# Three steps regrouped ahead of the score writes, and unused products on TensorE in the opening of a talking-heads attention and expert-layer kernel

## The chip, the cores and the metric

One core of one Trainium2 chip runs the whole program. The metric is the device time of one execution in microseconds (us). Five engines work side by side, each through its own list of instructions in order: TensorE (PE; its weight loads are shown apart as PEld), VectorE (DVE), ScalarE (ACT), GpSimd (POOL, here only an issuer of DMAs) and SyncE (SP, an issuer of DMAs). Sixteen DMA engines move the data.

## The reference

Inputs are q, k and v of shape (4, 12, 448, 64), two 12x12 head mixers, and the weights of two layers. In short:

```
scores = q @ k^T / 8                       # per batch and head, 448 x 448
scores = einsum("bhij,hg->bgij", scores, w_pre)
attn   = softmax over j of scores
attn   = einsum("bhij,hg->bgij", attn, w_post)
x      = (attn @ v) as 1792 rows x 768
x      = ((x @ w1) * (x @ w2)) @ w3 @ w_out
out    = max(x @ m1, x @ m2, x @ m3) @ m_out
```

The result is float32. The dense products are made from operands cut into a high and a low part (`hi`, `lo`), three products for each.

## The kernel before, in words

**Scores.** `unit(b, r, u)` (L331) multiplies 128 query rows (block r) of one pair of heads u with the keys `kall` into a PSUM room ("m", "p" or "s"), and ACT or DVE copies it out with the scale. For batch 0, block 0 the copies go to one wide row tile, `at` (called `a` in the trace, its six parts `("arow", u)`), all others to one of two tiles `st` (called `s`), and from both a DMA on SP writes them to `sdram`. The write of `at` leaves out the first FIRST rows (L365).

**Regrouping.** The head mixers need rows ordered by (query, head). `regroup(b, p)` (L373) builds the tile `x` of step p, 20 queries of 12 heads. It reads `sdram` with two DMAs, except for steps below FIRST of batch 0, which it copies out of `at` directly with four DMAs of 5 queries x 12 heads, 60 rows of 1792 bytes each (L384). There are three `x` tiles (AHEAD + 1).

**Steps.** `softmax` (L396) mixes heads on PE (`m<-x,kp`, L407), takes the negated maximum on DVE (`nmax`, L411) and the exponential on ACT (L414). `post` (L430) mixes again (L445) and copies the result into `at` over the rows; so this copy is planned after all readers of the rows. `attend` (L467) multiplies with v.

**Fusion and dense layers.** `fuse_parts` (L564) multiplies w3 with w_out (L605), in groups of 24 products (four pieces of six) that end in one of two PSUM banks `pw`; the first group uses `pw[0]`, the second `pw[1]`. Its operands arrive as 64-bit floats by DMAs of POOL and are made into float32 pairs by ACT and DVE (`convert`, L503, then L570/L571 for w_out and L535/L537 for w3). Six w_out buffers (`early`) and three w3 buffers (`wraw`) go round, so a load waits for a conversion. Dense layers for batches 0 and 1 follow between the attention steps (L685), and the last two batches come at the end (L221).

**The order.** Every piece is given to a planner (`Plan`, L67) with an engine, a cost, a key and what it reads and writes. `order` (L89) simulates the engines: each takes its ready piece with the lowest key; a load is started when the simulated pipe is less than BACK = 2.5 us behind, at RATE = 0.29 MB per us and LAND = 2.0 us to land; at most 8 loads of an engine are in flight. The instructions are emitted in that order, so each engine's list is fixed in advance, and a piece that is late on the chip holds what stands behind it on its engine. The pieces of the opening come from `attention_parts` (L1045): keys and queries, six units of block 0, then the regroups of the first two steps (L1063), then the second block of queries (L1065), then the loop over steps.

Of the kernel before, what the change touches and what calls it, by code (L numbers as in the profile page):

```python
# [18 lines left out]
P = 128  # L19
GI = 10  # L20
# [10 lines left out]
AHEAD = 2  # L31
# [3 lines left out]
HP = H // 2  # L35
# [22 lines left out]
SWITCH = 0.21  # L58
LAND = 2.0
RATE = 0.29  # L60
FIRST = 2 * 2 * GI
BACK = 2.5
STAY = 0.5
QUEUED = 8
# [2 lines left out]
class Plan:  # L67

    def __init__(self):
        self.ops, self.wrote, self.read = [], {}, {}  # L70

    def __call__(self, eng, took, key, do, reads=(), writes=(), bytes=0, mode=None):
        deps = set()
# [15 lines left out]
    def order(self):  # L89

        n = len(self.ops)
        after, left = [[] for _ in range(n)], [0] * n
        for x, op in enumerate(self.ops):
            left[x] = len(op[3])
            for d in op[3]:
                after[d].append(x)
        ready = {e: [] for e in ENGINES}
        loads = []
        busy = {e: False for e in ENGINES}
        taken, out, events = [False] * n, [], []  # L100
        mode, pipe = None, 0.0
        flying = {e: 0 for e in ENGINES}

        def offer(x):
            if self.ops[x][4]:
                heapq.heappush(loads, (self.ops[x][1], x))
                return
            for e in self.ops[x][0]:
                heapq.heappush(ready[e], (self.ops[x][1], x))

        for x in range(n):
            if not left[x]:
                offer(x)
        now, wake = 0.0, -1.0
        while True:
            later = []
            while loads and pipe - now < BACK:
                key, x = heapq.heappop(loads)
                (e, took), = self.ops[x][0].items()
                if busy[e] or flying[e] == QUEUED:  # L120
                    later.append((key, x))
                    continue
                busy[e] = True
                flying[e] += 1
                out.append((x, e, now))
                pipe = max(pipe, now + took) + self.ops[x][4] / RATE / 1e6
                heapq.heappush(events, (now + took, 0, x, e))
                heapq.heappush(events, (pipe + LAND, 1, x, None))
            for y in later:
                heapq.heappush(loads, y)  # L130
            if loads and pipe - now >= BACK and wake <= now:
                wake = pipe - BACK + 0.01
                heapq.heappush(events, (wake, 2, -1, None))
            for e in ENGINES:
                while not busy[e] and ready[e]:
                    if e == "PE":
                        best = min(ready[e], key=lambda r: (r[0] + STAY * (self.ops[r[1]][5] != mode), r[1]))
                        ready[e].remove(best)
                        heapq.heapify(ready[e])
                        x = best[1]  # L140
                    else:
                        _, x = heapq.heappop(ready[e])
                    if taken[x]:
                        continue
                    taken[x] = True
                    took, m = self.ops[x][0][e], self.ops[x][5]
                    if e == "PE" and m != mode:
                        took, mode = took + SWITCH, m
                    busy[e] = True
                    out.append((x, e, now))  # L150
                    heapq.heappush(events, (now + took, 0, x, e))
                    heapq.heappush(events, (now + took, 3, x, e))
                    heapq.heappush(events, (now + took + HOP, 1, x, e))
            if not events:
                break
            now, kind, x, e = heapq.heappop(events)
            if kind == 1 and self.ops[x][4]:
                flying[next(iter(self.ops[x][0]))] -= 1
            if kind == 0:
                busy[e] = False  # L160
            elif kind != 2:
                for y in after[x]:
                    same = e is not None and not self.ops[y][4] and list(self.ops[y][0]) == [e]
                    if same == (kind == 3):
                        left[y] -= 1
                        if not left[y]:
                            offer(y)
        assert len(out) == n, (len(out), n)
        self.end = now
        return out  # L170

# [6 lines left out]
def attention_talking_heads_moe_kernel(  # L178
# [16 lines left out]
    nc = tc.nc  # L195
# [128 lines left out]
    def load_q(b, r, key, eng="SP", after=()):  # L324
# [3 lines left out]
            3072 * w, list(after), [("q", slot)])  # L328
        return slot

    def unit(b, r, u, slot, key, room="s"):  # L331

        whole = P * (r + 1) <= S
        parts = [(u, 0), (u, HB)] if whole else [(2 * u, 0), (2 * u + 1, 0)]
        pt = {"m": pm, "p": pp, "s": pz}[room]

        w = min(P, S - P * r)
        q = qs[slot].rearrange("p x j -> p (x j)")[:, :HP * w].rearrange("p (x j) -> p x j", x=HP)

        def multiply(_):  # L340
            for c, (pr, i) in enumerate(parts):
                for o in range(2):
                    sl = slice(o * D, (o + 1) * D)
                    nc.tensor.matmul(  # L344
                        pt[HB * c:HB * c + HB, o, :S], q[sl, pr, i:i + HB], kall[sl, pr], start=True, stop=True
                    )

        bank_of = [(room, x) for x in range(2)]
        plan("PE", 0.76, key, multiply, [("k", pr) for pr, _ in parts] + [("q", slot)], bank_of, mode="q")
        if r == 0 and b == 0:  # L350
            out, where = at.rearrange("p t h i -> p (t h i)")[:, 2 * S * u:2 * S * (u + 1)], ("arow", u)
            out = out.rearrange("p (o j) -> p o j", o=2)
        else:
            n = turn("s", 2)
            out, where = st[n], ("st", n)

        def evict(e):
            if e == "ACT":
                nc.scalar.activation(out, pt[:, :, :S], AF.Copy, scale=D ** -0.5)
            else:  # L360
                nc.vector.tensor_scalar_mul(out, pt[:, :, :S], D ** -0.5)  # L361

        plan({"ACT": 0.95, "DVE": 1.12}, 0, key + 0.05, evict, bank_of, [where])
        if whole:
            x = 0 if r or b else FIRST  # L365
            dma("SP", key + 0.06, sdram[b][P * r + x:P * r + P, 2 * u:2 * u + 2], out[x:], 3584 * (P - x), [where],
                [("sd", b, r, u)])
        else:
            for c, (pr, _) in enumerate(parts):
                dma("SP", key + 0.06, sdram[b][P * r:S, 2 * pr:2 * pr + 2], out[HB * c:HB * c + HB], 229e3,  # L370
                    [where], [("sd", b, r, pr)])
# [192 lines left out]
    def fuse_parts():  # L564
# [30 lines left out]
        for m, n in jobs:  # L595
# [3 lines left out]
            for x in range(KH // 2):  # L599

                def multiply(_, x=x, n=n, b=b, hi=hi, lo=lo):
                    for k in (2 * x, 2 * x + 1):
                        oh, ol = o_tiles()[n][k]
                        for i, (w, r) in enumerate(((hi[:, k], oh), (hi[:, k], ol), (lo[:, k], oh))):
                            nc.tensor.matmul(pw[b][:, :FW], w, r, start=(k == 0 and i == 0),  # L605
                                             stop=(k == KH - 1 and i == 2))

                plan("PE", 1.06, fuse_at(j), multiply,
                     [("sh", g, x // 2), ("sl", g, x // 2)] + [("O", n, k) for k in (2 * x, 2 * x + 1)]
                     + [("Oh", n, k) for k in (2 * x, 2 * x + 1)], [("w", b)], mode="d")  # L610
                yield fuse_at(j)
                j += 1
# [137 lines left out]
    def tail_parts(pool_users, at_):  # L750
# [11 lines left out]
                groups.append([last.tile([P, 2 * HW], F32R, tag=x, name=x, bufs=2) for x in ("vhi", "vlo")])  # L762

        n = plan("SP", 0.0, at_(0), move, (), [("moved",)])
        plan.ops[n][3].update(pool_users)
        for x, src in enumerate((kept["a", 0], sums["a", 0][:, :2 * HW])):
            to = lambda x=x: groups[x][1].bitcast(F32)
            reads = [("kept", ("a", 0)), ("sums", "a", 0)][x:x + 1]
# [264 lines left out]
    def fuse_at(j):  # L1033
        return 3.0 + 20.0 * j / 64
# [10 lines left out]
    def attention_parts():  # L1045
# [5 lines left out]
        block_diagonals(-19.0)  # L1051
        for u in range(HP):
            unit(0, 0, u, slot, -8.0 + 0.1 * u, "mps"[u % 3])
        todo = [(0, r, u, (0.5 * u, 3 + u, 8.5 + 0.5 * u)[r - 1])
                for r in range(1, 4) for u in range(HP if r < 3 else 3)]
        for b in range(1, B):
# [3 lines left out]
            due.setdefault(int(s), []).append((b, r, u))  # L1060
        slots = {}
        xn = {}
        for s in range(AHEAD):  # L1063
            xn[s] = regroup(*steps[s], -7.0 + 0.1 * s)
        slots[0, 1] = load_q(0, 1, -5.6, after=[("arow", 2)])  # L1065
        yield -1.0
        en = {}
        for s in range(LAST + LAG):
            if s == 1:
                load_v(0, 3.0, [("arow", 5)])  # L1070
            for d in (s + 2,):
                for b, r, u in due.get(d, []):
                    if u == 0 and (b, r) not in slots:
                        slots[b, r] = load_q(b, r, s)
                    if u == 0 and r == 0 and b:
                        for x in range(0, HP, 2):
                            load_k(b, [x, x + 1], s + 0.1 * x)
            if s + AHEAD < LAST:
                xn[s + AHEAD] = regroup(*steps[s + AHEAD], s - 0.5)
            for x, (b, r, u) in enumerate(due.get(s, [])):  # L1080
                unit(b, r, u, slots[b, r], s + 0.5 * x)
# [100 lines left out]
```

## Time and profile before

| | us |
|---|---|
| Median of 3 runs | 1144.06 (1140.52 to 1148.41) |
| Profiled execution | 1145.06 |
| Its span | 1143.3 |
| PE busy | 1102.1 (96%) |
| DVE busy | 782.7 (68%) |
| ACT busy | 566.2 (50%) |

The span is cut in 40 slices on the page, and PE is busy nine tenths or more in all but a few of them. The ones that are not lie in the first two slices, where the granted clock is 0.8 and 0.7 as well, and in single places later. The profiled execution is 1.00 us above the median, and 1.76 us of it lie outside its span.

### The profile page before, as it was taken

What the parts mean: (1) busy time and instruction counts of PE and PEld (TensorE: products, weight loads), DVE (VectorE), ACT (ScalarE), POOL (GpSimd) and SP (SyncE); (2) the same over time, 40 slices, a digit from 0 to 9 for tenths busy, and PEclk for the clock granted to TensorE, in tenths of its full rate; (3) what the DMA queues carried; (4) which work ended last, traced back from release to release, by engine and by line L of the source; (5) the groups of instructions that cost most, each with busy time, mean ns of one, the idle gap of its engine ahead of it and who ended that gap; (6) DMA issues with size and microseconds to landing.
All of it is one profiled execution on the core that took longest, in us unless ns stands there. A gap on an engine that the chain in (4) does not pass through costs nothing.

```text
span 1143.3 us, 29211 instructions
## 1 busy us (share of the span) xinstructions
PE 1102.1 (96%) x12348; PEld 889.4 (78%) x12348; DVE 782.7 (68%) x1343; ACT 566.2 (50%) x1071; POOL 73.6 (6%) x141
## 2 busy tenths in 40 slices
PE   3999999999999999999999989998999999999998
PEld 1466777787877877777777868887988899888877
DVE  3666785686766777767576676774877764587874
ACT  4576475566654677655445353533433343333331
POOL 3100010000000000000110101100000000000000
PEclk8799999999999999999999999999999999999999
DMA  8798887989874999888899898856433421233343
GB/s 305 217 334 247 282 292 256 311 297 319 303 260 155 311 332 303 291 268 283 284 312 316 271 308 267 283 195 222 148 117 97 120 77 46 76 99 116 107 115 117
DMA packets 106205, 258.95 MB, mean 226 GB/s; under 512 B 20278, under 2 KB 57162, under 8 KB 106074
## 3 DMA queue, kind: packets, MB, share of 16 engines
q1 hardware_dynamic: 88474, 175.79, 47.7%
q0 software_dynamic: 15584, 77.62, 20.5%
q10 hardware_dynamic: 2016, 3.67, 0.9%
q8 instruction: 97, 1.59, 0.6%
q14 instruction: 34, 0.28, 0.1%
HBM read 174.27 MB, written 81.91 MB: 224 GB/s over the span
## 4 chain that ended last, share of the span: by engine, by line
PE 84%; DMA 6%; issue 4%; DVE 3%; ACT 2%; POOL 0%; SPq 0%; DVEq 0%; ACTq 0%; POOLq 0%
PE w L685 28%; PE w L221 8%; PE p L445 7%; PE p L479 6%; PE p L221 6%; PE m L407 6%; PE w L605 6%; PE m L221 6%; PE s L221 5%; PE s L344 5%; DMA x<-a 1%; DMA sdram<-a 1%; DMA wc<-kept_b 1%; DMA vlo<-sums_o 1%; DMA wc<-kept_m 1%
## 5 line engine op out<-in xcount | busy, mean ns | idle before, releaser
L445 PEld LDWEIGHTS p<-kwr,e 60*64 60x64 f32 x5760 | 103.3, 137 | 45.3 <-issue 28.4
L411 DVE TENSOR_REDUCE nmax<-m 128x2 f32<-128x896 f32 (+1 forms) x92 | 100.1, 1088 | 53.7 <-PE m L407 53.2
L414 ACT ACTIVATE e<-m,nmax 128x448 f32<-128x448 f32 (+1 forms) x184 | 115.0, 633 | 36.6 <-DVE nmax L411 36.1
L407 PE MATMUL m<-x,kp 60*64 60x448 f32 x720 | 98.0, 565 | 16.7 <-DMA x<-a 13.0
L445 PE MATMUL p<-kwr,e 60*64 60x60 f32 x5760 | 106.4, 221 | 5.0 <-DVE xlo L489 2.9
L277 ACT COPY a<-p 128x480 f32<-128x480 f32 (+1 forms) x97 | 53.5, 574 | 93.5 <-PE p L445 84.9
L685 PE MATMUL w<-yhi,whi 128*128 128x448 f32 x216 | 83.3, 385 | 0.0
L685 PE MATMUL w<-yhi,wlo 128*128 128x448 f32 x216 | 79.4, 368 | 0.0
L685 PE MATMUL w<-ylo,whi 128*128 128x448 f32 x216 | 79.3, 367 | 0.0
L344 PE MATMUL s<-kall,q 64*64 64x448 f32 x640 | 79.0, 564 | 0.2 <-DVE s L361 0.2
L479 PEld LDWEIGHTS p<-a,v 128*64 128x64 f32 x1536 | 73.7, 137 | 5.9 <-issue 4.8
L479 PE MATMUL p<-a,v 128*64 128x120 f32 (+1 forms) x1536 | 77.6, 260 | 0.0
L685 PE MATMUL w<-xhi,whi 128*128 128x448 f32 x192 | 73.8, 384 | 0.0
L277 DVE COPY a<-p 128x480 f32<-128x480 f32 (+1 forms) x83 | 53.2, 652 | 29.9 <-ACT a L277 23.1
L685 PE MATMUL w<-xhi,wlo 128*128 128x448 f32 x192 | 70.2, 366 | 0.0
L685 PE MATMUL w<-xlo,whi 128*128 128x448 f32 x192 | 70.0, 365 | 0.0
L747 ACT CAST whi<-wlo 128x768 fp32r<-128x768 f32 x39 | 32.6, 835 | 73.6 <-DMA wlo<-sums_m 17.9
L685 PE MATMUL w<-hhi,whi 128*128 128x448 f32 x168 | 64.1, 382 | 2.6 <-ACT whi L660 1.8
L661 DVE TENSOR_TENSOR wlo<-wlo,whi 128x768 fp32r<-128x768 f32 (+1 forms) x52 | 52.8, 1015 | 20.1 <-ACT whi L660 19.8
L407 PEld LDWEIGHTS m<-x,kp 60*64 60x64 f32 x720 | 24.0, 135 | 53.7 <-issue 37.3
L685 PE MATMUL w<-hhi,wlo 128*128 128x448 f32 x168 | 61.5, 366 | 0.8 <-DVE wlo L661 0.8
L221 PE MATMUL p<-t,vhi 128*128 128x448 f32 x204 | 61.7, 372 | 0.5 <-DVE r L934 0.4
(237 smaller groups left out, 2531.3 us busy)
## 6 DMA issues: line engine op xcount, KB each, us to landing
x<-sdram SPq DMA_DIRECT2D x172, 210.0 KB
sdram<-s SPq DMA_DIRECT2D x66, 448.0 KB
wraw<-in_wm POOLq DMA_DIRECT2D x18, 768.0 KB, 7.1
wlo<-kept_m SPq DMA_DIRECT2D x27, 384.0 KB
wlo<-kept_w SPq DMA_DIRECT2D x18, 512.0 KB
wraw<-in_w3T POOLq DMA_DIRECT2D x16, 512.0 KB, 7.2
kept_m<-wc SPq DMA_DIRECT2D x18, 384.0 KB
wc<-kept_m POOLq DMA_DIRECT2D x18, 384.0 KB, 6.0
```

What stands on the lines that cost most here:

```text
L221: nc.tensor.matmul(out, w, r, start=(k == 0), stop=(k == 3 * n_k - 1))
L277: (nc.scalar.copy if e == "ACT" else ENG[e].tensor_copy)(out, src)
L344: nc.tensor.matmul(pt[HB * c:HB * c + HB, o, :S], q[sl, pr, i:i + HB], kall[sl, pr], start=True, stop=True)
L407: nc.tensor.matmul(pm[HB * c:HB * c + HB, u, :S], kp[sl], x[sl, c], start=True, stop=True)
L411: plan("DVE", 1.1, key + 0.01, lambda _: nc.vector.tensor_reduce(out=nmax[:r], in_=pm[:r, :, :S], axis=AX.X, op=ALU.max, negate=True), m_b ...
L414: plan("ACT", 0.85, key + 0.02, lambda _, u=u: nc.scalar.activation(e_[:r, u], pm[:r, u, :S], AF.Exp, bias=nmax[:r, u:u + 1], scale=1.0, a ...
L445: nc.tensor.matmul(pt[HB * side:HB * side + HB, c, t, :, u * GB:u * GB + m], e_[sl, u, j:j + HB], kwr[sl, u, :, :m], start=True, stop=True,)
L479: nc.tensor.matmul(pt[o * D:(o + 1) * D, x, pr % 3, :], vt[:, jc, h * D:(h + 1) * D], a[:, jc, h, :], start=(jc == 0), stop=(jc == JC - 1),)
L605: nc.tensor.matmul(pw[b][:, :FW], w, r, start=(k == 0 and i == 0), stop=(k == KH - 1 and i == 2))
L661: plan("DVE", 0.16 + 0.8 * f, key - 0.9, lambda _: nc.vector.tensor_sub(lo, t, hi.bitcast(F32)), h, l)
L685: nc.tensor.matmul(pw[w][:, :S], u, r, start=(k == 0 and i == 0), stop=(k == nk - 1 and i == 2))
L747: nc.scalar.copy(hi, t)
```

## The change

FIRST goes from 40 to 60, so that the first three steps are copied out of `at` and the rows written to `sdram` fall from 88 to 68 in each of six DMAs. These six writes are now put off (`later`) behind the regroups of three steps, with a higher key (by 1.5 instead of 0.06) and with all six row parts as what they read. The planner gets a list of spare pieces: 120 products of 128x128 keys with 128 columns of keys into `pw[1]`, read by nothing. It takes one whenever PE has nothing ready, once the first keys have landed and until the first piece of the second fused group is taken; those left over are not emitted.

```diff
-FIRST = 2 * 2 * GI
+FIRST = 3 * 2 * GI
...
+        self.spares, self.until = [], None
...
+        spares = self.spares
+        held = set(spares)
         for x in range(n):
-            if not left[x]:
+            if not left[x] and x not in held:
                 offer(x)
...
+            if not busy["PE"] and spares and not left[spares[0]] and not taken[self.until] and events:
+                x, *spares = spares
+                busy["PE"] = taken[x] = True
+                mode = None
+                out.append((x, "PE", now))
+                heapq.heappush(events, (now + self.ops[x][0]["PE"], 0, x, "PE"))
...
+    later = []
...
             x = 0 if r or b else FIRST
-            dma("SP", key + 0.06, sdram[b][P * r + x:P * r + P, 2 * u:2 * u + 2], out[x:], 3584 * (P - x), [where],
-                [("sd", b, r, u)])
+            reads = [where] if r or b else [("arow", y) for y in range(HP)]
+            later.append(lambda: dma(
+                "SP", key + (0.06 if r or b else 1.5), sdram[b][P * r + x:P * r + P, 2 * u:2 * u + 2], out[x:], 3584 * (P - x), reads,
+                [("sd", b, r, u)]))
+            if r or b:
+                later.pop()()
...
+                if plan.until is None and b:
+                    plan.until = len(plan.ops)
...
-        plan.ops[n][3].update(pool_users)
+        plan.ops[n][3].update(set(pool_users) - set(plan.spares))
...
+        for _ in range(120):
+            plan.spares.append(plan("PE", 0.22, 0.0, lambda _: nc.tensor.matmul(
+                pw[1][:P, :P], kall[:, 0, :P], kall[:, 0, :P], start=True, stop=True)))
+            plan.ops[-1][3].update(plan.wrote["k", 0])
...
-        for s in range(AHEAD):
+        for s in range(AHEAD + 1):
             xn[s] = regroup(*steps[s], -7.0 + 0.1 * s)
+        while later:
+            later.pop(0)()
         slots[0, 1] = load_q(0, 1, -5.6, after=[("arow", 2)])
...
-            if s + AHEAD < LAST:
+            if AHEAD < s + AHEAD < LAST:
                 xn[s + AHEAD] = regroup(*steps[s + AHEAD], s - 0.5)
```

## Rows read from the trace of the kernel before

**Rows 1.** Windows: length; busy (count) by engine; granted clock; DMA share; GB/s.
```profile
0.00:25.00 25.00, 7.29 (x48) 2.36 (x48) 10.14 (x21) 11.92 (x20) 9.69 (x21) 0.85 0.86 309
25.00:50.00 25.00, 22.91 (x132) 9.48 (x133) 12.53 (x28) 11.93 (x28) 1.60 (x3) 0.60 0.69 203
50.00:75.00 25.00, 21.15 (x119) 14.88 (x117) 21.43 (x46) 19.17 (x43) 5.29 (x10) 0.93 1.02 339
75.00:100.00 25.00, 25.00 (x518) 19.06 (x516) 12.88 (x27) 14.83 (x32) 1.05 (x2) 1.00 0.83 262
```

**Rows 2.** Chain of work that ended last, 0 to 80 us: start, duration, what.
```profile
12.52 9.44 DMA sdram<-a
...
26.97 12.89 DMA x<-a
...
41.66 2.22 PE w L605 x6
...
50.33 6.71 DMA wraw<-in_w3T
...
71.84 2.31 PE w L605 x12
```

**Rows 3.** Waits of PE, 12 to 42 us: total, times, longest.
```profile
PE m L407 <- DMA x<-a: 13.0, 2, 12.6
```

**Rows 4.** Timeline of SP's issues, 0 to 75 us: start, duration, engine, what, count.
```profile
8.24 6.06 SPq L272 DMA_DIRECT2D sdram<-a  x6
14.35 13.63 SPq L272 DMA_DIRECT2D x<-a  x8
28.02 1.06 SPq L272 DMA_DIRECT2D q<-in_qT  x1
29.14 1.11 SPq L272 DMA_DIRECT2D x<-sdram  x2
46.27 0.34 SPq L272 DMA_DIRECT2D sdram<-s  x1
```

**Rows 5.** DMA issues, 0 to 80 us: count, size of each, median time to landing.
```profile
early<-in_w_out POOLq DMA_DIRECT2D x16, 384.0 KB, 8.5
...
sdram<-a SPq DMA_DIRECT2D x6, 308.0 KB
...
x<-a SPq DMA_DIRECT2D x8, 105.0 KB
```

**Rows 6.** Instructions of tile x, 0 to 80 us: shortest, median, longest ns; first, last.
```profile
L272 SPq DMA_DIRECT2D x<-a x8: 721/836/2957, 14.4 to 27.0; - x8
```

**Rows 7.** Windows of one us: columns as in rows 1.
```profile
19.00:20.00 1.00, 0.00 (x0) 0.00 (x0) 0.41 (x3) 0.63 (x2) 0.00 (x0) 0.50 0.71 289
...
34.00:35.00 1.00, 0.93 (x3) 0.50 (x2) 1.00 (x4) 1.00 (x5) 0.12 (x1) 0.50 0.31 122
```

**Rows 8.** Timeline of PE: start, duration, what, count [idle before, releaser].
```profile
5.46 1.77 PE L344 MATMUL m<-kall,q 64*64 64x448 f32 x8 [5.46 <-DMA kall<-in_kT]
7.00 1.72 PE L344 MATMUL p<-kall,q 64*64 64x448 f32 x8
...
11.83 0.92 PE L344 MATMUL s<-kall,q 64*64 64x448 f32 x8
...
51.53 0.44 PE L605 MATMUL w<-hhi,whi 128*128 128x384 f32 x1 [0.61 <-ACT whi L535]
...
59.65 0.45 PE L605 MATMUL w<-yhi,whi 128*128 128x384 f32 x1 [0.90 <-ACT yhi L570]
...
62.22 0.69 PE L605 MATMUL w<-yhi,whi 128*128 128x384 f32 x1 [1.27 <-ACT t L277]
```

**Rows 9.** Window of the first attend, line 479 alone: PE and PEld busy.
```profile
95.44:100.53 5.09, 5.07 (x96) 4.84 (x96) 1.00 1.02 310
```

**Rows 10.** Timeline of DVE, 30 to 54 us: columns as in rows 8.
```profile
32.56 1.09 DVE L411 TENSOR_REDUCE nmax<-m 128x2 f32<-128x896 f32 x1 [10.20 <-PE m L407]
...
52.84 1.08 DVE L361 TENSOR_SCALAR s<-s 128x896 f32<-128x896 f32 x1
```

More of the change, by code (lines that the diff above doesn't have):

```diff
@@ L165, in order @@
                         left[y] -= 1
-                        if not left[y]:
+                        if not left[y] and y not in held:
                             offer(y)
-        assert len(out) == n, (len(out), n)
+        assert len(out) == n - len(spares), (len(out), n)
         self.end = now
```

## The prediction

> **What bounds the kernel now.** I first read the windows over the whole span, to see where PE is not full. From 75 us on PE is busy 25.00 of 25 us in nearly every window; the opening is where it is not: 7.29, 22.91 and 21.15 us of 25, at a granted clock of 0.85, 0.60 and 0.93 [rows 1]. So PE's own list sets the end, and what the opening gains or loses reaches the end almost one for one. Next I read the chain of waits through the opening. It runs over a write of rows to `sdram` (12.52 us, 9.44 long), then a row copy `x<-a` that is issued at 26.97 and takes 12.89 us, then PE, then a load of w3 at 50.33 (6.71 us) [rows 2]. The waits of PE say the same from its side: 13.0 us in two waits for `x<-a`, one of 12.6 [rows 3]. SP's timeline gives the reason: six writes of 308 KB go out from 8.24, and the eight copies of 105 KB behind them need 13.63 us to be issued from 14.35 on, though one takes 0.72 to 0.84 us when nothing holds it [rows 4 to 6].
>
> The reader should also see the share of the DMA engines. At 19 us, with the writes in flight, 0.71 of them work and move 289 GB/s. At 34 us, with copies of steps 0 and 1, a query load and two `x<-sdram` all issued and the last copy not landed before 39.86, only 0.31 work, at 122 GB/s [rows 2, 4, 7]. So the opening is short of a few engines, not of bandwidth: 0.31 of 16 is five, 0.71 is about eleven, and each moves some 25 GB/s (289/(0.71 x 16) = 25.4; 122/(0.31 x 16) = 24.6).
>
> **The change part by part.** The sum is against the profiled execution, 1145.06 us; that is 1.00 above the median.
>
> *Copies before writes.* All twelve copies need the six row parts, as the eight did, so the first goes out near 14.35. At 0.84 us each [rows 6] the fourth, which completes step 0, goes out 2.5 us later, and with about 2 to 4 us to land it is there at 19 to 22 us, where PE's wait ended at 25.33 for the first of them and DVE's maximum `nmax` started only at 32.56 [rows 3, 10]. Step 1 follows 3.4 us later, so near 25, instead of 39.86. What leaves the queue ahead of them is 6 x 315 kB. DMA work in all: the writes shrink by 6 x 72 = 430 kB, two `x<-sdram` of step 2 go (420 kB), four copies come (430 kB) on few engines. The second block of queries has only a planner's tie to row part 2 and a lower key than the w_out loads; with the writes no longer ready earlier than it, I expect it ahead of the copies on SP. Then it is no wait later; behind the writes it would be.
>
> *Writes behind the copies.* Nobody needs the rows in `sdram` before step 3. But two things stand behind these writes on SP: `x<-sdram` of step 3 and the `sdram<-s` writes that free the two `st` tiles. The third unit of block 1 cannot be copied out (DVE, 52.84 in the trace, rows 10) before the first `sdram<-s` has landed, which was issued at 46.27 [rows 4]. If all 16 engines served the writes, 6 x 244 kB would take 4 us, and this cover holds: price 0. The trace excludes that: the present writes run on about eleven engines [rows 7], so at the best 1.46 MB/(11 x 25.4) = 5.2 us, done by 32. If they had only the five of the copies, 11.5 us behind 10.2 us of copies (1.29 MB/127 GB/s), plus POOL's loads on the same engines: done at 40 to 47, and the third unit is about where it was. I charge 1 us, with ends 0 and 6.
>
> By the Trainium skill (DMA: Bandwidth & Descriptors, Why a DMA increments its semaphore by 16 and not by 1), a DMA runs on the largest number of engines up to 16 that divides the slowest dimension on both sides. That gives 11 for 88 rows and 5 for a copy of 5 queries by 60 rows, with which 0.71 and 0.31 agree [rows 7], but only 4 for 68 rows. By an estimate from that page the writes would take 14.4 us, and the charge of this part would be 6 us rather than 1.
>
> *The products.* Price of one: line 479 does 96 matmul instructions of 120 columns in 5.07 us [rows 9], two to a product, on half the array's width. If width costs double, 2 x 2 x 53 x 128/120 = 225 ns; if not, 113. I take 225, since weights of 128 columns have to be loaded too. At the low clock twice that: the first units start 1.5 us apart at the start and take 0.92 later, at a recorded 1.00 [rows 8]. How many: keys and queries are planned 393 kB/0.29 = 1.36 us apart, so seven stand before the first unit. That is 7 x 0.45 = 3.2 us on PE at its slowest moment; the warm-up comes as early as before, and a later unit waits for evictions anyway, so I charge 1.3 us to the first copy (ends 0 and 3.2). Before step 0 the planner sees PE empty for the six w_out loads and four copies that it lets through its pipe: (2.36 + 0.43)/0.29 + 2 = 11.6 us, less up to three early units of 0.95, so some 40 products, 9 us. With units done at 14.2 PE comes to step 0 at 26 to 27, later than its data (21), earlier than before (all four copies there only shortly before 32.56). So the products eat half of what the copies win: `nmax` near 28, **4.5 us earlier** (ends 0 and 11). Until the second group there is room for about 51.5 - 5.5 - 19 (units, three steps, a post, the first group at full clock) = 27 us, or 120 products; I take 105, 23.6 us. PE's list up to the second group is then 5.5 + 1.3 + 19 + 23.6 = 49.4 us without any wait, against 51.53 [rows 8]. So **the second group comes about 1.5 us earlier**, not 4.5.
>
> *Clock.* Between 25 and 44 us PE worked at half clock. Six fused products took 2.22 us at 41.66 where twelve take 2.31 later [rows 2]; that gain of 1.1 us a piece is inside the 49.4 above. What PE lost after the second group it may win in part: waits of 0.61, 0.90 and 1.27 us that end at 51.53, 59.65 and 62.22 [rows 8] come from conversions, which restart 4.5 us earlier while PE gains 1.5. I take 2 us for them, and 1 us for the piece at 62.22 that ran at the low clock after them (0.69 against 0.45 for its first product).
>
> **Sum:** -1.5 - 2 - 1 for these, +1 for the writes: -3.5, and some 0.5 us for one `x<-sdram` step less in SP's list before step 3: -4.0. 1145.06 - 4.0 = 1141.1, or against the median **1140**. The late parts of the plan are ordered anew by small shifts of ready times; I know of no sign for that and leave it to the range, 3 us either way (the three runs alone span 8).
>
> **The rivals.** *The writes crawl.* They sit on fewer engines than before and hold `sdram<-s` and step 3 back until after 50 us. For it: 0.31 at 34 us shows that DMAs of this form can be held to five engines, and all queues share them. Against: eleven served the present writes. On four engines they would take 1.46 MB/(4 x 25.4) = 14.4 us, after 10.2 us of copies and beside some eight POOL loads (3 MB, 7 us on each engine): 15.4 + 32 = 47 us, with stalls 55. Its place is the third unit's copy; it decides once the first `sdram<-s` lands later than 52; at 58 it costs about 6 us against now, less the 1 us at the low clock: 1144 + 5 = 1149. The page of the Trainium skill named above speaks for this case. The same end is reached on PE if the products cost 0.30 instead of 0.225 us (105 x 0.075 = 8).
>
> *The whole stall goes.* PE reaches step 0 with its data, at 21 to 22, as fewer products stand before it or they cost 113 ns: `nmax` 10 us earlier, conversions too, and the w3 load of 50.33 at 40. For it: 10.20 us idle on DVE ends with `nmax` [rows 10]. Against: the DMA share is 1.02 from 50 to 75 us and 0.86 in the first 25 [rows 1], so loads that start 10 us earlier land less than 10 earlier. Full -11, likely -10: 1134.
>
> *Nothing moves.* The copies land as late as now because five engines carry 12 x 107.5 kB beside POOL's loads, or PE comes no earlier: 1144. For it: these engines already carry 0.86 MB in 25 us. I count it with the forecast's neighbourhood.
>
> **How the numbers follow.** 0.48 for the forecast (1137 to 1143), 0.14 for nothing (1143 to 1146), 0.20 for the crawl (1146 to 1154), 0.18 for the whole stall (1129 to 1137). A range from 1131 to 1151 leaves about 2 in 10 out, split between the ends. About 1% (11.4 us) is what a measurement of this kernel can tell from no change: faster than 1132.6 takes the better half of the stall case and some luck, 0.12; slower than 1155.5 the worst crawl together with dear products, 0.06; within 0.82.
>
> **What would show it.** `x<-a` issued without gaps from about 15 us and no `sdram<-a` before them; the first mixing on PE at 26 to 27 and behind products rather than waiting for `x<-a`; granted clock 1.00 from 10 us to the second group; 100 or so products of some 0.22 us; the DMA share during the put-off writes, at 0.7 or at a quarter. I am wrong if PE waits for copies at step 0 as long as before, if the second group starts after 53 us, or if PE is not full from 65 us on.

## The result, and the profile after

The changed kernel takes **1157.85 us** (median of four runs, 1157.32 to 1160.34) against 1143.42 for the kernel before in four runs beside it: a ratio of 1.0137, 95% interval 1.0109 to 1.0165. It is slower. The forecast was 1140, in a range from 1131 to 1151. The profiled execution took 1157.32 us (span 1155.5) against 1145.06 (span 1143.3) before.

The windows of the kernel after (length; busy time and count of PE, PEld, DVE, ACT, POOL; granted clock; DMA share; GB/s) answer to [rows 1], and those of 1 us to [rows 7]:

```profile
0.00:25.00 25.00, 18.99 (x155) 13.98 (x156) 11.49 (x23) 13.09 (x22) 9.47 (x21) 1.00 0.75 255
25.00:50.00 25.00, 20.94 (x173) 14.64 (x172) 15.48 (x38) 14.80 (x34) 5.16 (x10) 0.86 0.63 201
50.00:75.00 25.00, 13.01 (x79) 9.31 (x77) 8.63 (x18) 8.71 (x20) 2.12 (x4) 0.80 0.69 250
75.00:100.00 25.00, 22.63 (x328) 15.41 (x331) 13.23 (x28) 14.20 (x30) 0.00 (x0) 1.00 0.83 264
...
41.00:42.00 1.00, 1.00 (x2) 0.00 (x0) 0.00 (x0) 0.00 (x0) 0.00 (x0) 0.50 0.32 113
...
45.00:46.00 1.00, 1.00 (x5) 1.00 (x5) 1.00 (x3) 0.88 (x3) 0.01 (x1) 0.50 0.27 109
...
62.00:63.00 1.00, 0.00 (x0) 0.00 (x0) 0.00 (x0) 0.00 (x0) 0.00 (x0) 1.00 0.26 107
```

PE is busier in the first 25 us (products) and emptier from 50 to 75: 13.01 us against 21.15. DVE does 8.63 us of work there against 21.43. The DMA engines, whose share was 1.02 there, are at 0.69. The last row is the middle of that hole: no compute engine works at all, and a quarter of the DMA engines move 107 GB/s, 107/(0.26 x 16) = 25.7 GB/s each. A quarter of 16 is four. At 41 us only copies move, as the trace's packets of 1792 bytes show, which are theirs; their last ends at 45.2. So the row of 45 us shows the put-off writes almost by themselves, since POOL issues no load before 45.99: they too keep a quarter of the engines busy.

SP's timeline of after (start, duration, engine, what, count) answers to [rows 4]:

```profile
1.64 0.43 SPq L281 DMA_DIRECT2D q<-in_qT  x1
15.55 17.07 SPq L281 DMA_DIRECT2D x<-a  x12
32.66 13.08 SPq L281 DMA_DIRECT2D sdram<-a  x6
45.85 2.25 SPq L281 DMA_DIRECT2D sdram<-s  x1
68.62 0.80 SPq L281 DMA_DIRECT2D x<-sdram  x2
```

The order is the one that the change asks for. The chain of waits (start, duration, what) runs through step 1's last copy and then through the first `sdram<-s`, which takes 23.77 us to land; before, the copies and a load of w3 stood there [rows 2]:

```profile
28.38 13.79 DMA x<-a
42.21 1.77 PE m L422 x2
...
45.85 23.77 DMA sdram<-s
69.64 0.93 ACT s L370
70.61 1.77 PE s L355 x8
```

Timelines of after for PE, then DVE and ACT (start, duration, engine, line, what, tiles, shape, count, [idle before, releaser]) answer to [rows 8] and [rows 10]:

```profile
6.01 3.35 PE L1072 MATMUL w<-kall 128*128 128x128 f32 x14 [6.01 <-DMA kall<-in_kT]
...
14.15 5.85 PE L1072 MATMUL w<-kall 128*128 128x128 f32 x50
...
27.88 0.98 PE L422 MATMUL m<-x,kp 60*64 60x448 f32 x8
...
40.34 1.68 PE L422 MATMUL m<-x,kp 60*64 60x448 f32 x2 [2.75 <-DMA x<-a]
42.21 1.75 PE L422 MATMUL m<-x,kp 60*64 60x448 f32 x2 [0.19 <-DMA x<-a]
...
52.91 0.44 PE L620 MATMUL w<-hhi,whi 128*128 128x384 f32 x1
...
70.61 1.77 PE L355 MATMUL s<-kall,q 64*64 64x448 f32 x8 [11.17 <-ACT s L370]
...
29.00 1.09 DVE L426 TENSOR_REDUCE nmax<-m 128x2 f32<-128x896 f32 x1 [1.26 <-PE m L422]
...
44.00 1.09 DVE L426 TENSOR_REDUCE nmax<-m 128x2 f32<-128x896 f32 x1 [8.08 <-PE m L422]
...
69.64 0.92 ACT L370 ACTIVATE s<-s 128x896 f32<-128x896 f32 x1 [13.58 <-DMA sdram<-s]
```

Step 0's maximum came 3.6 us earlier than before (32.56, [rows 10]). Step 1's, the second `nmax`, came 2.3 us later than in the kernel before, whose DVE timeline has:

```profile
41.69 1.09 DVE L411 TENSOR_REDUCE nmax<-m 128x2 f32<-128x896 f32 x1 [1.35 <-PE m L407]
```

DVE idled 8.08 us for it where it had idled 1.35: what was won at step 0 was gone at step 1. Between step 1 and the sixth step the loss grows to 12.3 us, and the span is 12.2 us longer. The sixth maximum, after and then before:

```profile
100.03 1.09 DVE L426 TENSOR_REDUCE nmax<-m 128x2 f32<-128x896 f32 x1 [1.62 <-PE m L422]
...
87.71 1.09 DVE L411 TENSOR_REDUCE nmax<-m 128x2 f32<-128x896 f32 x1 [0.41 <-PE m L407]
```

The third unit of block 1, copied out at 52.84 on DVE before [rows 10], is copied out at 69.64 on ACT: that copy writes an `st` tile which the first `sdram<-s` has to have read. ACT waits 13.58 us for it, PE 11.17 us behind ACT. POOL issues eight weight loads between 45.99 and 53.1 and then none until 72.65, because the conversions that free their tiles stand behind the waiting copy.

### The profile page after: what moved, and what is told of

Read it like the earlier page. It is cut to its first block, busy times and chain, and to the rows that moved or that the text cites. A ratio compares the mean times of both kernels' runs of the same rounds, so it can differ in the third digit from the quotient of the medians.

```text
span 1155.5 us, 29520 instructions
## 1 busy us (share of the span) xinstructions
PE 1113.2 (96%) x12514; PEld 908.7 (79%) x12514; DVE 787.4 (68%) x1351; ACT 561.4 (49%) x1063; POOL 74.0 (6%) x141
## 4 chain that ended last, share of the span: by engine, by line
PE 87%; DMA 6%; DVE 3%; ACT 2%; SPq 1%; issue 0%; DVEq 0%; ACTq 0%; POOLq 0%
PE w L702 31%; PE w L230 8%; PE p L460 7%; PE p L494 7%; PE p L230 6%; PE m L422 6%; PE m L230 6%; PE s L230 6%; PE s L355 5%; PE w L620 5%; DMA sdram<-s 2%; DMA x<-a 1%; SPq L281 1%; DMA vlo<-sums_o 1%; DMA wc<-kept_m 1%
## 5 line engine op out<-in xcount | busy, mean ns | idle before, releaser
L460 PE MATMUL p<-kwr,e 60*64 60x60 f32 x5760 | 103.9, 219 | 4.8 <-DVE xlo L504 3.1
L286 ACT COPY a<-p 128x480 f32<-128x480 f32 (+1 forms) x96 | 53.1, 574 | 96.8 <-PE p L460 86.5
L422 PE MATMUL m<-x,kp 60*64 60x448 f32 x720 | 94.8, 560 | 4.1 <-DMA x<-a 4.1
L286 DVE COPY a<-p 128x480 f32<-128x480 f32 x84 | 53.7, 651 | 29.6 <-ACT a L286 16.8
L543 DVE SCALAR_TENSOR_TENSOR wc<-wc,wraw 128x768 uint32<-128x768 uint32 (+1 forms) x56 | 48.8, 877 | 24.4 <-ACT wc L540 24.2
L764 ACT CAST vhi<-vlo 128x384 fp32r<-128x384 f32 (+1 forms) x39 | 25.9, 670 | 75.2 <-DMA vlo<-sums_m 26.1
```

The costliest lines, as they stand in the source:

```text
L286: (nc.scalar.copy if e == "ACT" else ENG[e].tensor_copy)(out, src)
L422: nc.tensor.matmul(pm[HB * c:HB * c + HB, u, :S], kp[sl], x[sl, c], start=True, stop=True)
L460: nc.tensor.matmul(pt[HB * side:HB * side + HB, c, t, :, u * GB:u * GB + m], e_[sl, u, j:j + HB], kwr[sl, u, :, :m], start=True, stop=True,)
L764: nc.scalar.copy(hi, t)
```

## The experiments

Four kernels test the row count and the products apart; they share one set of runs of the kernel before (1142.1). Each ratio below is the one on record with its runs; it can differ from the quotient of the two medians by up to 0.15%.

**80 rows instead of 68.** The put-off writes take 12 rows more, with the same bytes in the planner's account, so that each engine's instructions keep their order.

```diff
-            x = 0 if r or b else FIRST
+            x = 0 if r or b else 48
...
-"SP", key + (0.06 if r or b else 1.5), ..., 3584 * (P - x), reads,
+"SP", key + (0.06 if r or b else 1.5), ..., 3584 * (P - (x and FIRST)), reads,
```

> The changed kernel, every instruction in the same place; only the six put-off writes take 80 rows (from row 48) instead of 68 (from row 60), so each moves 18% more. Theory A (68 rows run on four DMA engines, and the third unit's copy on ScalarE waits for them): 80 rows run on all sixteen; the first sdram<-s lands before 55 us instead of 69.6, the idle stretch of PE from 59 to 70 us goes, 1138 to 1148 us against 1157.85. Theory B (the writes are late because they stand behind twelve slow copies on SP's queue, whatever they run on): more bytes, so as late or later, 1157 to 1163. Theory C (the products on TensorE cost the time): 1157, no change.

Measured: 1147.39, ratio 1.0037 [1.0015, 1.0059]. A window of 1 us with the writes in flight, the chain of waits, and ACT's timeline:

```profile
45.00:46.00 1.00, 1.00 (x5) 1.00 (x5) 1.00 (x4) 0.91 (x4) 0.57 (x1) 0.50 0.81 258
...
27.30 14.31 DMA x<-a
...
56.32 0.92 ACT L370 ACTIVATE s<-s 128x896 f32<-128x896 f32 x1 [0.53 <-DMA sdram<-s]
```

More bytes, in less time: the unit's copy waits 0.53 us instead of 13.58 and comes at 56.32, a little later than the 55 expected. At 45 us, where 68 rows moved 109 GB/s at a share of 0.27, 80 rows move 258 at 0.81. Step 1's last copy lands about as late as in after (27.30 + 14.31 = 41.6).

**76 rows**, by the same edit with 52 for 48.

> The changed kernel, only the six put-off writes take 76 rows (from row 52) instead of 68, 12% more bytes. Theory A: 76, like 68, leaves four engines; the DMA share stays at 0.25 while they run alone and the first sdram<-s lands 2 to 3 us later, 1159 to 1162. If it were the number of rows or bytes in some smooth way, 76 would lie near the run with 80 rows, in either direction.

Measured: 1157.63, ratio 1.0137 [1.0106, 1.0169]. Its window of 1 us and ACT's timeline:

```profile
45.00:46.00 1.00, 1.00 (x5) 1.00 (x4) 1.00 (x3) 1.00 (x4) 0.39 (x1) 0.50 0.26 108
...
70.75 0.92 ACT L370 ACTIVATE s<-s 128x896 f32<-128x896 f32 x1 [15.35 <-DMA sdram<-s]
```

Eight rows more than after change nothing, not even the 2 to 3 us that were expected for their bytes; four more than these take 10.2 us off (1157.63 to 1147.39). So it is not the bytes. That it is what divides the number of rows, and not where the rows begin, is settled further down by the writes of 64 and 4 rows.

**No products** (68 rows).

```diff
-        for _ in range(120):
+        for _ in range(0):
```

> The changed kernel without the products on TensorE (none of 120), regroups and put-off writes as they are. Theory A: PE waits in the same place for the third unit's copy, the first sdram<-s lands at 65 to 70 us, 1152 to 1160; the granted clock falls to its lower level before step 0. Theory C: the time goes back to 1140 to 1146.

Measured: 1154.34, ratio 1.0110 [1.0091, 1.0130]. SP's, PE's and ACT's timelines:

```profile
13.33 17.70 SPq L281 DMA_DIRECT2D x<-a  x12
...
25.37 1.47 PE L422 MATMUL m<-x,kp 60*64 60x448 f32 x8
...
69.93 0.92 ACT L370 ACTIVATE s<-s 128x896 f32<-128x896 f32 x1 [14.74 <-DMA sdram<-s]
```

The products cost 3.5 us here (against the 1157.85 of the first set). The copies go out 2.2 us earlier without the seven products that stand in front of the first unit; the stall of the third unit is unchanged.

**80 rows and no products.**

> 80 rows in the put-off writes and no products. Theory A: no idle stretch at 59 to 70 us, step 0 on PE at 20 to 24 us instead of 27.9; beside the run with 80 rows and the products it shows what the products are worth: 1134 to 1146, within 4 us of that run. Theory C: clearly faster than that run, by 6 us or more.

Measured: 1142.55, ratio 1.0007 [0.9985, 1.0029]. With both removed, what is left of the change (three steps regrouped, the writes put off) moves nothing. Step 0 came to PE at 25.48, later than the 20 to 24 expected. By the four runs the row count costs 11.8 us without products and 10.2 with them (76 rows), the products 3.5 and 4.8: 0.45 + 4.84 + 10.24 = 15.5 us over the kernel before for the 76-row kernel, by the path 1142.1, 1142.55, 1147.39, 1157.63.

**The kernel before with the products alone**: the reserve of 120 products, its rule in the planner and its limit from the diff, nothing else.

> The kernel before with the products alone (two steps copied, writes of 88 rows first, as before). Theory A (the products are an own small cost: 83 of them at 0.234 us stood on TensorE in the changed kernel, part of them in front of work that was ready): 3 to 5 us over the kernel before, 1145 to 1148, though the granted clock stays at its upper level where it fell before. Rival (the clock they hold pays for them, and they only cost where the writes crawl): 2 to 4 us under it, 1138 to 1140.

Measured: 1148.68 against 1142.99, ratio 1.0041 [1.0016, 1.0065]. Products alone make the kernel before slower, by 5.7 us between the medians and 4.7 by the ratio, a little more than the 3 to 5 expected. PE's timeline:

```profile
29.93 1.45 PE L416 MATMUL m<-x,kp 60*64 60x448 f32 x8
...
43.32 1.75 PE L416 MATMUL m<-x,kp 60*64 60x448 f32 x2 [1.89 <-DMA x<-a]
```

Step 0 was mixed by 31.4, step 1's last piece only from 43.32 to 45.07; its `nmax` followed at 45.11, 3.4 us later than before.

**The kernel before with 96 rows in its early writes** instead of 88, order unchanged.

```diff
-            x = 0 if r or b else FIRST
+            x = 0 if r or b else 32
```

> The kernel before, every instruction in the same place; only its six early writes take 96 rows (from row 32) instead of 88. Theory A (88 rows run on eleven engines, 96 on sixteen; per engine 129 kB instead of 172): the DMA share at 17 to 22 us rises from 0.7 to 0.9 or more, step 0 is on PE 2 to 4 us earlier than 25.3; the copies that follow stay on five engines, so step 1 comes 1 to 2 us earlier; 0 to 3 us faster than before, 1139 to 1142. If engines did not matter here: 9% more bytes, 0 to 1 us slower.

Measured: 1144.47, ratio 0.9998 [0.9975, 1.0021]. The window that showed 0.71 and 289 GB/s before [rows 7]:

```profile
19.00:20.00 1.00, 0.00 (x0) 0.00 (x0) 0.69 (x2) 0.43 (x2) 0.00 (x0) 0.50 1.02 414
```

The writes go from eleven engines to all 16, and the time stays: step 0's `nmax` came at 28.33, 4.2 us earlier, and step 1's at 43.84, 2.2 us later, where 1 to 2 us earlier was expected. Speed in the write is not what the opening lacks.

**After without products, one step copied**: only step 0 is copied from the row parts, 112 rows are put off behind four copies, steps 1 and 2 are read back from `sdram`.

```diff
-FIRST = 3 * 2 * GI
+FIRST = 2 * GI
...
+            x = 0 if r or b else 16
...
         for s in range(AHEAD + 1):
             xn[s] = regroup(*steps[s], -7.0 + 0.1 * s)
-        while later:
-            later.pop(0)()
+            while later:
+                later.pop(0)()
```

> The changed kernel without products, with only step 0 copied (FIRST one step, four copies), the put-off writes behind these four and with 112 rows (from row 16), and steps 1 and 2 read back from sdram. Theory A (copies sit on five engines and are the last thing that step 1 waits for; writes and reads on fifteen or sixteen are cheap): step 0 at 21 to 24 us, step 1 before 37 us instead of 39.5 to 42; 1130 to 1140. Rival (the way through sdram has its own two landings, 6 to 9 us): step 1 at 38 to 42 and 1141 to 1146.

Measured: 1145.2, ratio 1.0024 [1.0002, 1.0047]. Its window while copies are in flight (POOL issues one load in the second half of it), and DVE's timeline:

```profile
18.00:20.00 2.00, 0.43 (x4) 0.30 (x8) 2.00 (x3) 1.47 (x3) 0.54 (x1) 0.50 0.26 48
...
52.02 1.09 DVE L426 TENSOR_REDUCE nmax<-m 128x2 f32<-128x896 f32 x1 [14.83 <-PE m L422]
```

Here copies move 48 GB/s in all, 48/(0.26 x 16) = 11.5 GB/s an engine, where the prediction took 127 GB/s for five engines. At this rate twelve of 107.5 kB would need 27 us, and in after their packets run from 17.1 to 45.2; but it is not their only rate, since at 41 us of after they move 113 GB/s. The expectation failed: step 1 was to come before 37 us and the time to fall to 1130 to 1140. Its `nmax` came at 52.02, 10.3 us later than before, because `x<-sdram` had to wait for the put-off writes; and yet the time rose by only 0.2%.

**After without products, two steps copied** (88 rows put off, as many steps regrouped as in the kernel before; only the order differs from it).

> The changed kernel without products and without the third step: two steps copied, then the put-off writes with 88 rows. Theory A: the writes run on eleven engines, the third unit of block 1 waits little, 1138 to 1145, some 10 us under the run without products at 68 rows (1154.34). Rival (putting the writes off is itself the cost): 1149 to 1156.

Measured: 1145.01, ratio 1.0016 [0.9993, 1.0038]. DVE's timeline:

```profile
40.26 1.09 DVE L426 TENSOR_REDUCE nmax<-m 128x2 f32<-128x896 f32 x1 [6.96 <-PE m L422]
```

Step 0's `nmax` came at 27.61 and step 1's at 40.26, 5.0 and 1.4 us earlier than before, and the time is no better. Copies before writes buy nothing by themselves.

**After with each put-off write issued as 64 and 4 rows.**

```diff
+            for z in (slice(0, 64), slice(64, P - FIRST)):
+                ENG[e].dma_start(out[z], src[z])
```

> The changed kernel with its products and its planned order; each of the six put-off writes of 68 rows is issued as two DMAs, 64 rows and 4 rows, so the bytes are the same to the row. Theory A (the number of engines, set by what divides the row count, is the whole cost): the first sdram<-s lands before 57 us, 1143 to 1150, as the run with 80 rows (1147.39). Rival (80 rows was fast for another reason, such as where its rows begin): 1155 to 1160. Six more issues on SP cost it 2 us at most.

Measured: 1148.42 against 1141.95, ratio 1.0055 [1.0037, 1.0073]. Same rows, same bytes, products included. ACT's timeline:

```profile
58.33 0.92 ACT L376 ACTIVATE s<-s 128x896 f32<-128x896 f32 x1 [2.44 <-DMA sdram<-s]
```

Nearly all of the row count's cost is gone with two issues in place of one; the copy comes at 58.33, a little later than the 57 expected.

**The kernel before with one step copied**: 112 rows written first, four copies, steps 1 and 2 read back.

```diff
-FIRST = 2 * 2 * GI
+FIRST = 2 * GI
...
-            x = 0 if r or b else FIRST
+            x = 0 if r or b else 16
```

> The kernel before with only step 0 copied; the early writes, first as before, take 112 rows (from row 16), steps 1 and 2 are read back from sdram. Theory A (a copy is what is slow: some 2.5 us each on five engines): step 0 near 25 us, step 1 at 30 to 35 instead of 39.9 to 41.7, 1134 to 1142. Rival (the opening is held by the volume of loads and conversions, so that steps 0 and 1 earlier change nothing): 1141 to 1145.

Measured: **1136.85** against 1141.95, ratio 0.9958 [0.9938, 0.9978]: faster than both kernels. SP's and PE's timelines:

```profile
8.40 6.44 SPq L272 DMA_DIRECT2D sdram<-a  x6
14.89 4.20 SPq L272 DMA_DIRECT2D x<-a  x4
...
23.42 2.18 SPq L272 DMA_DIRECT2D x<-sdram  x2
...
23.91 1.72 PE L407 MATMUL m<-x,kp 60*64 60x448 f32 x2 [10.64 <-DMA x<-a]
...
34.31 3.57 PE L407 MATMUL m<-x,kp 60*64 60x448 f32 x8 [0.86 <-DMA x<-sdram]
```

Four copies are issued in 4.20 us, where eight took 13.63 [rows 4]; step 1 is mixed at 34.31 and its `nmax` comes at 37.96, 3.7 us earlier than before. The sixth comes 3.7 us earlier as well:

```profile
84.06 1.09 DVE L411 TENSOR_REDUCE nmax<-m 128x2 f32<-128x896 f32 x1 [1.68 <-PE m L407]
```

**The kernel before with no copies** (`FIRST = 0`: all rows written, all steps read back).

> The kernel before without any copy: 128 rows in the early writes, all steps read back from sdram. Theory A: steps 0 and 1 wait for two landings but on fifteen and sixteen engines; step 0 at 25 to 30, step 1 at 28 to 34, 1133 to 1142. Rival (the volume holds the opening): 1141 to 1146.

Measured: 1138.8 against 1141.95, ratio 0.9961 [0.9942, 0.9981]. DVE's timeline has the first two maxima and the sixth:

```profile
34.47 1.09 DVE L411 TENSOR_REDUCE nmax<-m 128x2 f32<-128x896 f32 x1 [2.21 <-PE m L407]
...
38.07 1.09 DVE L411 TENSOR_REDUCE nmax<-m 128x2 f32<-128x896 f32 x1
...
81.68 1.09 DVE L411 TENSOR_REDUCE nmax<-m 128x2 f32<-128x896 f32 x1 [0.41 <-PE m L407]
```

Step 0's comes 1.9 us later than before, step 1's 3.6 earlier, both later than expected (steps at 25 to 30 and 28 to 34), and the kernel is faster: step 0 is not the point that the end hangs on. The order differs too: three units of block 1 stand ahead of step 0 here.

**The one-step kernel with 40 products** in one block between the sixth unit and step 0.

> The kernel before with one step copied and 112 rows in the early writes (1136.85 us), and 40 products, all of them between the sixth unit and step 0, where TensorE waits for copies from 13 to 23.9 us. At 0.234 us they end near 23, before the data. Theory A (products cost only where they stand in front of work that is ready; what the higher clock saves on TensorE in the opening is mostly hidden by waits): granted clock 1.00 when step 0 starts, step 0 done 2 to 3 us sooner, whole time 1134 to 1138. Rival (the clock is worth its own microseconds all through to the second group): 1130 to 1133. Rival (products cost wherever they are): 1139 to 1142.

Measured: 1142.49 against 1143.04, ratio 1.0004 [0.9990, 1.0017]. PE's timeline:

```profile
12.14 9.20 PE L1066 MATMUL w<-kall 128*128 128x128 f32 x80
...
34.14 1.75 PE L416 MATMUL m<-x,kp 60*64 60x448 f32 x2 [2.35 <-DMA x<-a]
```

The gain of the one-step kernel is gone; 1134 to 1138 was expected if products cost only in front of work that is ready, 1139 to 1142 if they cost wherever they are. But this run does not say why: the products end at 21.3, well before step 0's last copy (34.14, against 30.8 at the latest without them), and the planner put some conversions in another order. It is inconclusive on what a product costs where PE would have waited anyway.

## Why the prediction was wrong, step by step

**The failed step is *Writes behind the copies***, charged 1 us with ends 0 and 6; it costs 10 to 12. Two of its numbers failed. It took five to eleven engines, the nearest rows of the trace, for a write of a shape that the trace did not have; the put-off writes ran on four, as 0.27 at 45 us shows, and 80 rows or 64 and 4 rows take most of the cost away. And it let the copies end near 25, so that even the rival on four engines was done by 47, with stalls 55. Step 1's last landed at 42.2, the last of all at 45.2. From 42.2 the same working, an estimate, gives the stall: each of the four engines had 0.37 MB of rows to move, 0.22 MB of the eight loads of 384 and 512 KB that POOL issued from 46 to 53, and 0.03 MB of `sdram<-s`; 0.62 MB at 25 GB/s is 25 us, to 67. It landed at 69.6. The trace's packets show the sharing: at 62 us those of the writes (3584 bytes) and those of the w3 loads (4096 bytes) move half of the 107 GB/s each. How much of the stall is the writes' and how much the loads' share behind them was not tested apart.

The Trainium skill (DMA: Bandwidth & Descriptors, Why a DMA increments its semaphore by 16 and not by 1) has the rule of the divisor, and the trace agrees for 68 rows (0.27), 76 (0.26), 88 (0.71) and 96 (1.02). With 80 rows the 0.81 at 45 us is thirteen engines on the average, which fits 16 that were not always busy. The prediction quoted the rule, and charged the trace's nearest row.

**The rival *the writes crawl*** had the place (the third unit's copy) and the mechanism right; the 55 to 58 that it gave for the landing and its 1149 were too small, for the two reasons above and because it left products out of its price.

***Copies before writes*** was mis-sized too, with no step to lose by it but the gain. The price of 0.84 us a copy is the time to issue one when nothing holds the queue, and 122 GB/s at 34 us [rows 7] had a query load and two reads from `sdram` in it besides. The row that held the price was the other one: eight copies in 13.63 us of issue, landed by 39.86. By the packets of after, the copies moved 47 GB/s from 17 to 22 us, nearly alone; only 23 from 28 to 38 us, while POOL's weight loads (packets of 4096 and 6144 bytes) moved 241 on all the engines, the copies' among them; and 113 at 41 us, alone. Why they were slow at first is not shown; that they then shared their engines with the loads is the reason that the rival *nothing moves* gave. Step 1's last piece started at 42.21 (39.52 with 80 rows and no products), so none of the 15 us expected for it came, and the 3.6 us that step 0 won were lost again there. The queries did go ahead of the copies (1.64).

***The products.*** One costs 2 x 5.85/50 = 0.234 us where 0.225 was taken; 83 were issued, not 105; step 0 reached PE at 27.88 where 26 to 27 was forecast, and `nmax` 29.00 where 28 was. They were costed as filling empty time. Seven in front of the first unit delay the copies by 2.2 us (13.33 to 15.55; 1.9 in the pair with 80 rows), within the bound of 3.2 and above the 1.3 charged. In all they cost 3.5 to 4.8 us, and 5.7 in the kernel before, between medians. Which of the later ones cost the remainder stays open; the run of 40 in one block did not settle it. The prediction's own sum has a slip here: 49.4 against 51.53 is 2.1 us, where it took 1.5.

***The second group*** started at 52.91, 1.4 us after 51.53 and not 1.5 before it, just short of the 53 that was named as a sign; PE was not full from 65 us on, which was named too. The 3 us counted for waits and the low clock from 51.53 to 62.22 can be set against no number, since the stall lies there now. ***Clock***: 1.00 through the first 40 us as forecast, but it fell to half near 40.4 after a wait for copies, and again near 64.3 after some five idle us; filler that the plan lays out in time did not cover waits which the plan did not have.

***The whole stall goes*** and ***nothing moves*** did not occur in the changed kernel (of the latter only its reason for late copies), though 80 rows without products are the latter to 0.07%.

What bounds the opening stays open. The maxima of the first, second and sixth step on DVE, read from each kernel's timeline, against the ratio:

| kernel | step 0's `nmax` | step 1's `nmax` | sixth `nmax` | ratio |
|---|---|---|---|---|
| before, one step copied | 30.82 | 37.96 | 84.06 | 0.9958 |
| before, no copies | 34.47 | 38.07 | 81.68 | 0.9961 |
| before, 96 rows | 28.33 | 43.84 | 89.74 | 0.9998 |
| before | 32.56 | 41.69 | 87.71 | 1 |
| before, one step copied, 40 products | 35.93 | 40.89 | 83.10 | 1.0004 |
| after, 80 rows, no products | 26.96 | 41.31 | 85.98 | 1.0007 |
| after, two steps copied, no products | 27.61 | 40.26 | 87.75 | 1.0016 |
| after, one step copied, no products | 28.71 | 52.02 | 90.89 | 1.0024 |
| after, 80 rows | 28.77 | 43.44 | 89.34 | 1.0037 |
| before, with products | 31.41 | 45.11 | 91.34 | 1.0041 |
| after, 64 and 4 rows | 29.13 | 43.70 | 90.63 | 1.0055 |
| after, no products | 26.91 | 42.05 | 98.88 | 1.0110 |
| after | 29.00 | 44.00 | 100.03 | 1.0137 |
| after, 76 rows | 28.13 | 43.62 | 100.88 | 1.0137 |

The time does not follow step 0, which the change was about in the prediction. It does not follow step 1 either: step 1 came 10.3 us later with one step copied behind put-off writes, for 0.2% of time, and 1.4 us earlier with two, for no gain. It goes better with the sixth maximum, though not in every row: with 40 products that came 4.6 us earlier and the time is that of before.

The prediction's premise, that what the opening gains or loses reaches the end almost one for one, can be followed through the profiles. It holds for the changed kernel, 12.3 us late at the sixth maximum with a span 12.2 us longer, and for the one without copies, 6.0 us early there, 6.1 at the 91st maximum of 92, with a span 5.9 us shorter. It does not account for the one-step kernel: that is 3.7 us early at the sixth maximum, 0.6 at the 46th and 9.0 at the 91st, with a span 9.5 us shorter. Between 600 and 800 us PE idles 6.1 us before and 1.2 there. So more than half of that profile's lead arises far behind the opening; no run here shows why.

## What to carry to other kernels

Before a slice of a DMA changes size, see how many engines the new number of rows gets by what divides it, and keep a count that 16 divides, by some rows more or by a second small issue: 12 rows more took 10 us off here. Before a transfer is put off, list what stands behind it on its queue and which buffer that frees, and price a copy by the time from its issue to its landing with its neighbours in flight, not by its shortest issue. Filler on an engine with an ordered list delays whatever is planned behind it, so it wants a place where no released work can stand behind it, and a measurement of its own. To see whether a gain in the opening lasts, follow it to a point behind the opening: here the first two steps said little about the end, and the sixth said more.

## What the runs showed of the hardware

- Writes of 68 and 76 rows used a quarter of the 16 DMA engines (0.27 and 0.26 at 45 us, 109 and 108 GB/s), those of 96 rows all of them (1.02, 414 GB/s). Behind the six of 68 rows, with eight weight loads issued beside it, a write of 128 rows and 448 KB on the same queue landed 23.77 us after its issue.
- Copies of 5 queries by 60 rows between tiles, with hardly another transfer in flight, moved 48 GB/s at a share of 0.26 in one place (18 to 20 us, one step copied) and 113 at 0.32 in another (41 us of after); what made the difference was not found. Writes of rows moved 25 to 26 GB/s an engine.
- A float32 product of 128 x 128 x 128 ran as two instructions, 0.117 us each at a granted clock of 1.00.
